# Clearing a scratch tile on GpSimd behind row scatters, and moving a small copy to GpSimd, in a fused FFT filter and mixture-of-experts kernel

## The chip, the cores and the metric

The kernel runs on one core of a Trainium2 chip. The metric is the device time of one execution in microseconds (us). The core has five engines with a program each: TensorE (PE in the profile, its weight loads PEld), VectorE (DVE), ScalarE (ACT), GpSimd (POOL), and SyncE (SP), which here only issues DMA transfers.

## The reference

```python
# x: 8 sequences of 2496 rows of 256; filt: 1249 frequencies of 256
X = np.fft.rfft(x, axis=1)
y = np.fft.irfft(X * (filt_r + 1j * filt_i)[None], n=2496, axis=1)
# 19968 rows go to the one of 8 experts that has the largest logit
logits = y.reshape(19968, 256) @ w_gate
expert_idx = np.argmax(logits, axis=1)
probs = softmax(logits)
for e in range(8):
    mask = expert_idx == e
    h = np.maximum(y[mask] @ w1[e], 0.0)        # 256 -> 1024
    out[mask] = probs[mask, e] * (h @ w2[e])    # 1024 -> 256
```

Everything is float32. Each sequence is filtered along its length, each of its rows is given to one expert, and the expert's two layers are computed on that row alone.

## The kernel before

**The filter.** A sequence of 2496 = 39 x 64 rows is transformed by matrix products, in halves of 128 columns (16 units, two to a sequence). Each unit has five steps t of four small spectra (80 steps in all): transposes on PE (`spec1`, L312), a product by twiddle matrices (`spec2`, L327), the multiplication by the filter on DVE (`filt_`, L346 to L348), the addition of its two parts (`join`, L356, on GpSimd for t < 71, on DVE behind that), and the product back (`spec3`, L367), which ACT copies out (L372). Two scatters of 117 rows each make a pair; a sequence has 11 pairs. For each pair PE transposes (`inv1`, L634, ACT copies to `gh`, L640) and multiplies (`inv2`, L649, ACT copies to `yt`, L651), and `inv3` sends the rows to their expert's place.

**The routing.** `route1` to `route6` work out a sequence's logits, the chosen expert, the gate and the row's place `dest` in a big DRAM array `xs`, sorted by expert. The routing data of each row (`meta`: a tiny constant, the reciprocal of the softmax sum, the row's number) travel with it in four more columns. So a row of `xs` has 260 values of float32. `inv3(b, j, gg)` copies the `meta` of a pair into the last four columns of `yt` (117 x 2 x 4 values, L658, once for a pair) and issues one indirect DMA (L158, `scatter`) for each of its two groups. That makes 22 scatters a sequence, 176 in all. Behind the last sequence eight more scatters (`tail`) fill up each expert's last block with empty rows.

**The experts.** `xs` is worked off in blocks of 128 rows, in three segments: 16 blocks as soon as sequences 0 to 5 lie in `xs` (8 units of two blocks that share an expert's weights), 48 blocks when sequence 7 does (24 units of two), and the rest (up to 99 units of one). A block is loaded (`load`, SP; the first load of a segment waits for all scatters that it needs), scaled (`prep`, DVE, L1048 to L1057), split into two halves of float16 (`split`, ACT L1062 and DVE L1063), transposed by DMA (`turn`, L1070), multiplied by the first layer's weights (`layer1`, 48 matmuls, L1083, with ACT L1089 and L1091 and DVE L1097 in `halves`), by the second's (`layer2`, 24 matmuls, L1109, DVE L1119), scaled by its gate (`out_`, ACT L1125) and scattered to `out` by one more indirect DMA of 128 rows (`send`, also L158). Weights are fetched (`loadw`, L1021, 1 MB each for `wa` and `wb`) when the expert changes. 161 blocks are written out, two stand under a condition and are empty in this run.

**The order.** The order on every engine is set by hand: `at(time, function)` puts each step on a list, which is sorted by its time (in spectral steps t) and issued in this order.

```python
at(t + K["si"] * rho, join, t)
at(t + K["s3"] * rho, spec3, t)
...
z = max(z + 1.2 * c, s0 + c * RT[9] + 0.1 + 0.9 * d * j)
for gg in range(2):
    at(z + 0.45 * d * gg, inv3, b, j, gg)
...
at(nx + 0.95 * dx + 0.5, send, b)
...
for _, f, a in sorted(work, key=lambda w: w[0]):
    f(*a)
```

The first 16 blocks are put among the spectral steps of the last sequences (`PLACE[0]` = 80.9), so that between about 430 and 580 us GpSimd issues scatters of sequences 5 to 7 and of the first blocks' outputs by turns.

Of the kernel before, what the change touches and what calls it, by code (L numbers as in the profile page):

```python
# [9 lines left out]
F32 = mybir.dt.float32  # L10
# [11 lines left out]
S, D, E, F = 2496, 256, 8, 1024  # L22
# [91 lines left out]
def tile_fft_moe(ctx, tc, x, filt_r, filt_i, w_gate, w1, w2, cst, out):  # L114
    nc = tc.nc
    B = x.shape[0]
# [7 lines left out]
    SEG = []  # L124
# [14 lines left out]
    cp = ctx.enter_context(tc.tile_pool(name="cp", bufs=1))  # L139
    ident = cp.tile([128, 128], F32, name="ident")  # L140
    small = cp.tile([128, 64], F32, name="small")
    zrow = cp.tile([128, ROW], F32, name="zrow")
    rbase = cp.tile([128, E], F32, name="rbase0")
    tbs = [cp.tile([128, 4], I32, name=f"tb{i}") for i in range(len(SEG))]
    nblk = cp.tile([128, 1], I32, name="nblk")
# [3 lines left out]
    def free(inst, own, *others):  # L149
        ins = inst.ins  # L150
        for g in (*others, own):
            tc.declare_no_dep(ins, group=g, reason="every row is written once")
        tc.add_to_no_dep_group(own, ins)
        writers.setdefault(own, []).append(ins.name)

    def scatter(dst, idx, src, bound, *groups):
        free(
            nc.gpsimd.indirect_dma_start(  # L158
                out=dst,
                out_offset=bass.IndirectOffsetOnAxis(ap=idx, axis=0),  # L160
                in_=src,
                in_offset=None,
                bounds_check=bound,
                oob_is_err=False,
            ),
            *groups,
        )

    def after(ins, names):
        for name in names:  # L170
            tc.add_manual_dep(
                ins,
                name,
                mybir.DependencyInfo(
                    mybir.DependencyClass.Sync, mybir.DependencyReason.DATA
                ),
                reason="the rows are dispatched",
            )
# [6 lines left out]
    with ExitStack() as fctx:  # L185
# [468 lines left out]
        def inv3(b, j, gg):  # L654
            yt = sti[b, j] if gg == 0 else sti.pop((b, j))
            dest, meta = rst[b]
            if gg == 0:
                nc.vector.tensor_copy(yt[:, :, D:], meta[:, 2 * j : 2 * j + 2])  # L658
            g = 2 * j + gg
            scatter(  # L660
                xs[:, :], dest[:, g : g + 1], yt[:, gg], E * NP - 1,
                f"s{b}", "ld", *(f"s{i}" for i in range(b)),
            )

        def blocks(rb, up, nm):

            t8 = lambda n, dt=F32: rp.tile([128, E], dt, name=nm + n, tag="t" + n)
            ci = t8("ci", I32)
            nb = t8("nb")
            nc.vector.tensor_tensor(nb, rb, small[:, 0:8], op=ALU.subtract)  # L670
            nc.vector.tensor_scalar(ci, nb, up, None, op0=ALU.add)
            nc.vector.tensor_scalar(ci, ci, 7, None, op0=ALU.arith_shift_right)
            nc.vector.tensor_copy(nb, ci)
            return nb
# [168 lines left out]
        def tail(e):  # L843
            scatter(
                xs[:, :], rst["tail"][:, e : e + 1], zrow, E * NP - 1,
                "z", "ld", *(f"s{i}" for i in range(B)),
            )


        K = {"s2": 1.394, "sr": 1.65, "si": 1.85, "s3": 3.6, "f": 0.063, "fd": 0.75, "w": 6.0, "wp": 4.1}  # L850
# [29 lines left out]
        for b in range(B):  # L880
# [26 lines left out]
            for j in range(NPAIR):  # L907
                z = s0 + lead + j * d
                at(z, inv1, b, j)
                at(z + 0.7 * c, inv2, b, j)  # L910
# [3 lines that stand above are left out]
# [9 lines left out]
            if b == B - 1:  # L923
                at(last + 0.1, tails)
                for e in range(E):
                    at(last + 1.2 + e, tail, e)
# [27 lines left out]
        home = []  # L954
# [173 lines left out]
        def send(b):  # L1128
            ot, t = st.pop(b)
            scatter(out[:, :], t, ot, N - 1, "out")  # L1130

# [33 lines left out]
        for b in range(NB):  # L1167
            z, d, s = tau[b]
            y = max(opened(s) + 0.3, z - (1.1 if b else 1.45))
            at(y, prep, b)  # L1170
            at(y + 0.05, split, b)
            at(y + 0.1, turn, b)
            at(z, layer1, b, 0)
            at(z + 0.2 * d, halves, b, 0)
            at(z + 0.25 * d, layer1, b, 1)
            at(z + 0.45 * d, halves, b, 1)
            nx, dx = (tau[b + 1][0], tau[b + 1][1]) if b + 1 < NB else (z + d, d)
            at(nx + 0.5 * dx, layer2, b, 0)
            at(nx + 0.75 * dx, layer2, b, 1)
            at(nx + 0.95 * dx, out_, b)  # L1180
            at(nx + 0.95 * dx + 0.5, send, b)
# [5 lines left out]
        with tc.If(n > NFIN - NREST):  # L1187
            for k in range(nu, len(units)):
                load(k)
                loadw(k, 0)  # L1190
                loadw(k, 1)
            for b in range(NB, NBLK):
                prep(b)
                split(b)
                turn(b)
            for b in range(NB, NBLK):
                for i in range(2):
                    layer1(b, i)
                    halves(b, i)
            for b in range(NB, NBLK):  # L1200
                layer2(b, 0)
                layer2(b, 1)
                out_(b)
                send(b)
# [32 lines left out]
```

## Time and profile before

| | |
|---|---|
| time before, median of 3 runs | 1393.22 us (1393.07 to 1394.41) |
| the profiled execution's own time | 1391.01 us |
| its span, first to last instruction | 1389.2 us |
| mean granted TensorE clock | 0.986 |
| busy: PE / PEld / DVE / ACT / POOL | 1313.8 / 1177.2 / 831.5 / 842.3 / 470.7 us |
| chain that ended last, by line | PE `ph` L1083 24%, PE `po` L1109 24%, DMA `wb` 3%, issue 2% |
| software DMA queue (the scatters) | 19472 packets, 42.51 MB, 12.1% of 16 engines' span |

Busy time is the time in which an engine executes an instruction. The chain is the work that ended last, followed back from the last instruction to what released each step. The granted clock is the share of TensorE's full speed that it was allowed. The 1.8 us between time and span lie ahead of the first and behind the last instruction.

### The profile page before, as it was taken

To read this page: it belongs to the slowest core of one execution; us is meant where nothing else is said; L and a number is where in the kernel's file an instruction comes from. 1 tells how busy PE (TensorE), PEld (TensorE's weight loads), DVE (VectorE), ACT (ScalarE), POOL (GpSimd) and SP (SyncE) were. 2 spreads that over 40 slices of the span, in tenths; PEclk is the share of its full clock that TensorE was granted. 3 is DMA by queue.
4 is the path that set the end of the run, shared out by engine and by line. 5 is a ranking of instruction groups with operands and counts; after the bars stand their busy time and mean duration, and the time that the engine had idled before them with its cause. 6 is when DMAs were issued, how large, how long until landed. Compare 5 with 4: busy or idle time off the path is not lost.

```text
span 1389.2 us, 38966 instructions
## 1 busy us (share of the span) xinstructions
PE 1313.8 (95%) x14855; PEld 1177.2 (85%) x14855; DVE 831.5 (60%) x2400; ACT 842.3 (61%) x1444; POOL 470.7 (34%) x446
## 2 busy tenths in 40 slices
PE   6799999999989899899999999999999999999997
PEld 5778777777877677789999999889999999999997
DVE  1698879888887464255555555555555555555552
ACT  3567667676766555455666665556656565656564
POOL 3638576485664433323111111111111111111111
PEclk9999999999999999999999999999999999999999
DMA  9746565565542722496878878573554546373731
GB/s 173 200 158 206 167 195 178 162 210 171 184 144 81 177 76 79 142 302 172 221 211 212 221 200 248 140 190 73 151 118 106 166 103 167 77 196 73 192 79 43
DMA packets 201438, 220.95 MB, mean 159 GB/s; under 512 B 104359, under 2 KB 177690, under 8 KB 190178
## 3 DMA queue, kind: packets, MB, share of 16 engines
q1 hardware_dynamic: 181310, 175.21, 45.9%
q0 software_dynamic: 19472, 42.51, 12.1%
q8 instruction: 118, 1.93, 0.6%
q10 hardware_dynamic: 468, 0.72, 0.2%
q14 instruction: 70, 0.57, 0.1%
HBM read 335.66 MB, written 61.56 MB: 286 GB/s over the span
## 4 chain that ended last, share of the span: by engine, by line
PE 48%; DMA 5%; issue 2%; DVE 1%; ACT 1%; SPq 1%; POOL 0%; POOLq 0%; ACTq 0%
PE ph L1083 24%; PE po L1109 24%; DMA wb<-wscr 3%; DMA wa<-wscr 1%; DVE bm L1097 1%; DMA T<-xs 0%; POOL out_dram L158 0%; ACT hs L1089 0%; ACT T L1091 0%; DMA xb<-xs 0%; DVE m L1048 0%; ACT xs L1062 0%; SPq L1070 0%; SPq L973 0%; DVE xs L1063 0%
## 5 line engine op out<-in xcount | busy, mean ns | idle before, releaser
L1083 PE MATMUL ph<-T,wa 128*128 128x128 f16 x7728 | 463.8, 220 | 14.1 <-issue 7.4
L1083 PEld LDWEIGHTS <-wa 128*128 128x128 f16 x7728 | 447.5, 98 | 27.2 <-issue 15.6
L1109 PE MATMUL po<-wb,T 128*128 128x256 f16 x2576 | 433.6, 274 | 6.6 <-DMA wb<-wscr 3.6
L1097 DVE TENSOR_TENSOR bm<-hs,T 128x512 f16<-128x512 f32 x322 | 222.7, 692 | 352.8 <-ACT T L1091 308.1
L158 POOL DMA_INDIRECT out_dram<-ot,t x161 | 157.2, 977 | 649.0 <-DVE xs L1063 567.1
L1109 PE MATMUL po<-wb,bm 128*128 128x256 f16 x1288 | 352.2, 273 | 0.0
L1109 PEld LDWEIGHTS <-T 128*128 128x128 f16 x2576 | 246.3, 98 | 38.2 <-issue 7.5
L1089 ACT ACTIVATE hs<-ph 128x512 f32<-128x512 f32 x322 | 191.6, 595 | 104.5 <-PE ph L1083 77.0
L158 POOL DMA_INDIRECT xs<-yt,dest x176 | 186.3, 1059 | 149.8 <-issue 45.7
L1062 ACT ACTIVATE xs<-xb,s 128x256 f16<-128x256 f32 x161 | 81.8, 508 | 226.3 <-DVE s L1052 224.0
L1091 ACT CAST T<-hs 128x512 f16<-128x512 f32 x322 | 199.0, 618 | 10.1
L1109 PEld LDWEIGHTS <-bm 128*128 128x128 f16 x1288 | 126.5, 98 | 15.2
L356 POOL TENSOR_TENSOR p<-tr,ti 128x512 f32<-128x512 f32 x71 | 95.4, 1344 | 85.2 <-DVE ti L348 78.3
L372 ACT COPY U<-pi 128x512 f32<-128x512 f32 (+1 forms) x80 | 87.4, 1093 | 48.9 <-PE pi L367 41.7
L1063 DVE SCALAR_TENSOR_TENSOR xs<-xb,s,xs 128x256 f16<-128x256 f32 x161 | 78.0, 485 | 59.3 <-ACT xs L1062 57.5
L649 PE MATMUL py<-gh,dm 117*117 117x512 f32 x176 | 94.0, 615 | 7.2 <-ACT gh L640 6.8
L367 PE MATMUL pi<-cm,p 128*128 128x128 f32 (+1 forms) x640 | 86.9, 279 | 10.3 <-POOL p L356 7.2
L264 PE MATMUL f<-a,x 117*128 117x117 f32 (+1 forms) x628 | 87.3, 277 | 5.6 <-DVE T L272 2.9
L327 PEld LDWEIGHTS px<-z,bm 128*128 128x128 f32 x640 | 80.0, 193 | 14.2 <-issue 11.5
L367 PEld LDWEIGHTS pi<-cm,p 128*128 128x128 f32 x640 | 79.0, 193 | 12.9 <-POOL p L356 7.9
L272 ACT COPY T<-f 128x468 f32<-128x468 f32 (+1 forms) x80 | 70.7, 884 | 30.5 <-PE f L264 28.8
L327 PE MATMUL px<-z,bm 128*128 128x128 f32 x640 | 87.1, 279 | 0.4 <-ACT U L372 0.4
(180 smaller groups left out, 1326.5 us busy)
## 6 DMA issues: line engine op xcount, KB each, us to landing
wb<-wscr SPq DMA_DIRECT2D x129, 1040.0 KB
wa<-wscr SPq DMA_DIRECT2D x129, 1024.0 KB
xb<-xs SPq DMA_DIRECT2D x161, 130.0 KB
wf<-in_moe_w_dram SPq DMA_DIRECT2D x32, 512.0 KB
x<-in_x_dram SPq DMA_DIRECT2D x210, 78.0 KB
wscr<-wh SPq DMA_DIRECT2D x8, 1040.0 KB
wscr<-wh SPq DMA_DIRECT2D x8, 1024.0 KB
xs<-yt,dest POOLq DMA_INDIRECT x176
```

Source lines behind the costliest of these rows:

```text
L158: nc.gpsimd.indirect_dma_start(out=dst, out_offset=bass.IndirectOffsetOnAxis(ap=idx, axis=0), in_=src, in_offset=None, bounds_check=bound, ...
L264: nc.tensor.matmul(ps[:, n : n + m], lhsT=xt.pop((u, g))[:m], rhs=a1[:m, :m], start=True, stop=True,)
L327: nc.tensor.matmul(ps[:, kk], lhsT=bm[:, 4 * it + kk], rhs=z[:, kk], start=True, stop=True,)
L356: e.tensor_tensor(p, tr, ti, op=ALU.add)
L367: nc.tensor.matmul(ps[:, o : o + n], lhsT=p[:, kk], rhs=cm[:, k, :n], start=True, stop=True)
L372: nc.scalar.copy(U[u % NU].rearrange("p n r -> p r n")[:, r0 : r0 + o // 64, :], ps[:, :o].rearrange("p (r n) -> p r n", n=N2),)
L649: nc.tensor.matmul(ps[:GP], lhsT=dm, rhs=gh[:GP], start=True, stop=True)
L1083: nc.tensor.matmul(ps[:, f], lhsT=w[:, p : p + 128], rhs=xt[:, r, c], start=(n == 0), stop=(n == 5))
L1089: nc.scalar.activation(s, ps, AF.Relu, scale=1.0 / B23)
L1091: nc.scalar.copy(hh, s)
L1097: nc.vector.tensor_tensor(hl, s, hh, op=ALU.subtract)
L1109: nc.tensor.matmul(ps, lhsT=h2[q][:, f % 4], rhs=wv[:, r, f], start=(f == 0 and n == 0), stop=(f == 7 and n == 2),)
```

## The change

A tile `pad` of 128 x 384 float32 is added. `pause()` clears it on GpSimd; nothing reads it. It is issued behind each scatter of sequences 6 and 7 (44), behind each of the eight `tail` scatters, and behind the output scatters of the blocks whose unit is one of the first eight (16 blocks, the first segment). The copy of `meta` into `yt` goes from DVE to GpSimd for all eight sequences (88 copies).

```diff
--- before.py
+++ after.py
@@ -140,6 +140,7 @@
     ident = cp.tile([128, 128], F32, name="ident")
     small = cp.tile([128, 64], F32, name="small")
     zrow = cp.tile([128, ROW], F32, name="zrow")
+    pad = cp.tile([128, 384], F32, name="pad")
     rbase = cp.tile([128, E], F32, name="rbase0")
     tbs = [cp.tile([128, 4], I32, name=f"tb{i}") for i in range(len(SEG))]
     nblk = cp.tile([128, 1], I32, name="nblk")
@@ -165,6 +166,9 @@
             ),
             *groups,
         )
+
+    def pause():
+        nc.gpsimd.memset(pad, 0.0)
 
     def after(ins, names):
         for name in names:
@@ -655,12 +659,14 @@
             yt = sti[b, j] if gg == 0 else sti.pop((b, j))
             dest, meta = rst[b]
             if gg == 0:
-                nc.vector.tensor_copy(yt[:, :, D:], meta[:, 2 * j : 2 * j + 2])
+                nc.gpsimd.tensor_copy(yt[:, :, D:], meta[:, 2 * j : 2 * j + 2])
             g = 2 * j + gg
             scatter(
                 xs[:, :], dest[:, g : g + 1], yt[:, gg], E * NP - 1,
                 f"s{b}", "ld", *(f"s{i}" for i in range(b)),
             )
+            if b >= B - 2:
+                pause()
 
         def blocks(rb, up, nm):
 
@@ -845,6 +851,7 @@
                 xs[:, :], rst["tail"][:, e : e + 1], zrow, E * NP - 1,
                 "z", "ld", *(f"s{i}" for i in range(B)),
             )
+            pause()
 
 
         K = {"s2": 1.394, "sr": 1.65, "si": 1.85, "s3": 3.6, "f": 0.063, "fd": 0.75, "w": 6.0, "wp": 4.1}
@@ -1128,6 +1135,8 @@
         def send(b):
             ot, t = st.pop(b)
             scatter(out[:, :], t, ot, N - 1, "out")
+            if home[b][0] < SEG[0][2]:
+                pause()
```

## Rows read from the trace of the kernel before

**Rows 1.** Part 1 of the page: busy us, share of the span, instructions.

```profile
PE 1313.8 (95%) x14855; PEld 1177.2 (85%) x14855; DVE 831.5 (60%) x2400; ACT 842.3 (61%) x1444; POOL 470.7 (34%) x446
```

**Rows 2.** Waits of PE's weight loads, 430 to 620 us: total us, times, longest.

```profile
PEld L1083 <- issue: 15.6, 28, 1.3
PEld L1109 <- issue: 6.2, 13, 2.2
```

**Rows 3.** The same view, 620 us to the end.

```profile
PEld L1109 <- issue: 1.3, 3, 0.7
```

**Rows 4.** Busy time by stretch: length, PE, PEld, DVE, ACT, POOL, PEclk, DMA, GB/s.

```profile
455.00:468.40 13.40, 8.51 (x42) 5.83 (x41) 7.95 (x23) 5.57 (x9) 6.36 (x7) 0.81 0.57 171
515.70:525.20 9.50, 5.73 (x37) 3.77 (x35) 1.75 (x8) 3.44 (x7) 3.81 (x4) 0.82 0.22 67
556.30:563.30 7.00, 4.55 (x46) 3.85 (x44) 0.78 (x2) 3.03 (x6) 1.97 (x2) 0.76 0.35 97
568.50:576.00 7.50, 4.62 (x31) 3.29 (x29) 1.24 (x3) 2.74 (x5) 2.04 (x3) 0.77 0.54 179
446.50:580.00 133.50, 117.26 (x1182) 95.48 (x1181) 66.31 (x265) 69.95 (x128) 56.92 (x56) 0.94 0.43 111
```

**Rows 5.** Timeline of PE, 514 to 523 us: start, length, instruction, idle before.

```profile
516.68 0.22 PE L1083 MATMUL ph<-T,wa 128*128 128x128 f16 x1 [0.34 <-issue]
...
521.66 0.37 PE L634 MATMUL pg<-ident,U 128*117 128x128 f32 x1 [0.43 <-issue]
```

**Rows 6.** Timeline of GpSimd (POOL), 505 to 524 us.

```profile
511.65 0.99 POOL L158 DMA_INDIRECT xs<-yt,dest  x1 [3.42 <-DMA xs<-yt,dest]
...
519.42 1.00 POOL L158 DMA_INDIRECT xs<-yt,dest  x1 [0.30 <-issue]
```

**Rows 7.** Timeline of GpSimd, 445 to 464 us.

```profile
446.52 0.99 POOL L158 DMA_INDIRECT xs<-yt,dest  x1 [16.32 <-ACT gh L640]
...
462.24 0.99 POOL L158 DMA_INDIRECT xs<-yt,dest  x1 [0.30 <-issue]
```

**Rows 8.** Timeline of GpSimd, 548 to 574 us.

```profile
550.95 0.99 POOL L158 DMA_INDIRECT xs<-yt,dest  x1 [3.59 <-ACT yt L651]
...
557.63 0.99 POOL L158 DMA_INDIRECT out_dram<-ot,t  x1 [0.30 <-issue]
```

**Rows 9.** GpSimd's groups by form: busy us, mean ns, idle before.

```profile
L809 POOL MEMSET go<- 128x176 f32 x1 | 0.2, 236 | 0.0
...
L805 POOL MEMSET wg<- 128x64 f32 x1 | 0.2, 151 | 0.0
```

**Rows 10.** VectorE's (DVE's) groups by form, the copy of line 658.

```profile
L658 DVE COPY yt<-meta 117x8 f32<-117x8 f32 x88 | 28.6, 331 | 0.5
```

**Rows 11.** Timelines of DVE and of GpSimd, 229 to 235 us.

```profile
230.69 1.71 DVE L658 COPY yt<-meta 117x8 f32<-117x8 f32 x1
...
231.06 1.30 POOL L356 TENSOR_TENSOR p<-tr,ti 128x512 f32<-128x512 f32 x1
233.24 1.00 POOL L158 DMA_INDIRECT xs<-yt,dest  x1 [0.88 <-issue]
```

**Rows 12.** Timelines of DVE, GpSimd and PE in sequence 1, 174 to 184 us.

```profile
176.17 0.68 DVE L348 TENSOR_TENSOR ti<-px,ff 64x512 f32<-64x512 f32 x1
...
175.65 1.30 POOL L356 TENSOR_TENSOR p<-tr,ti 128x512 f32<-128x512 f32 x1
177.15 1.00 POOL L158 DMA_INDIRECT xs<-yt,dest  x1 [0.19 <-DVE yt L658]
...
180.75 1.30 POOL L356 TENSOR_TENSOR p<-tr,ti 128x512 f32<-128x512 f32 x1
...
178.84 1.06 PE L367 MATMUL pi<-cm,p 128*128 128x128 f32 x8
```

**Rows 13.** Timeline of GpSimd, and the chain that ended last (start, us), 575 to 590.

```profile
579.22 0.99 POOL L158 DMA_INDIRECT xs<-yt,dest  x1 [0.30 <-issue]
...
586.89 3.66 DMA xb<-xs
```

## The prediction

> **What bounds the kernel now.** I began with the page. PE is busy for 1313.8 of 1389.2 us [rows 1], so an edit on GpSimd (POOL in the profile) can move the end only through time in which PE stands still or runs slowly. The second view is what the weight loads of PE waited for, once between 430 and 620 us, where the last two sequences and the first 16 blocks are interleaved, and once behind that. In the first stretch the layer 1 matmuls (L1083) lose 15.6 us in 28 waits labelled "issue", and those of layer 2 (L1109) another 6.2 us [rows 2]. "Issue" means that the profile shows nothing that PE waited for. In the 769 us behind it, with some 145 blocks of the same matmuls, only 1.3 us of such waits are left [rows 3]. So something belongs to the interleaved stretch alone.
>
> The third view, the timeline of PE, shows the form of such a wait: from 516.68 to 521.66 us single matmuls stand with idle time before each, where the layer's groups otherwise run without a gap [rows 5]. Next I laid GpSimd's timeline beside it. The stall from 515.7 to 521.7 lies inside a run of seven scatters from 511.65 to 519.42, one behind the other, 1.30 us apart (0.99 plus a gap of 0.30) [rows 6]. The other places with such matmuls have a run of scatters too: twelve from 446.52 to 462.24 [rows 7], six from 550.95 to 557.63 with six more close behind [rows 8]. Each stall begins some 4 to 9 us into the run and ends at most about 2 us behind it. Runs of three scatters have none. This is a coincidence in time, four times out of four; the profile names no cause.
>
> What these four places cost is read from one view, busy time by stretch [rows 4]. PE idle: 13.40 - 8.51 = 4.89, 9.50 - 5.73 = 3.77, 7.00 - 4.55 = 2.45, 7.50 - 4.62 = 2.88, together 14.0 us. Behind each idle time the granted clock falls to the lower level for a few us, so the stretches average 0.81, 0.82, 0.76 and 0.77. Length times the missing share is 2.5 + 1.7 + 1.7 + 1.7 = 7.6 us. The four places hold 21.6 us, or 1.6% of the span, and the pauses are put at just these scatters.
>
> **The change part by part.** *The pause.* No memset of 128x384 stands in the trace. Two of the same kind took 236 ns for 176 elements and 151 ns for 64 [rows 9]: 0.76 ns an element, so 236 + 208 x 0.76 = 394 ns. There are 44 behind the scatters of sequences 6 and 7, 8 behind the tails and 16 behind the outputs of the first 16 blocks: 68 x 0.394 = 27 us on GpSimd. A scatter behind a compute instruction started after 0.19 us in place of 0.30 [rows 12], so the distance between two scatters goes from 1.30 to about 0.99 + 0.39 + 0.19 = 1.57 us. The direct cost on the path I set to 0 and bound it so. Between 446.5 and 580 us GpSimd is busy 56.9 of 133.5 us [rows 4]; 55 gaps of 0.30 make it 73 us. The 55 pauses there add 22 us and give back 55 x 0.11 = 6. What waits for the end of these scatters is the first load of the second segment, which is issued at 586.89 us behind the queue's own work [rows 13]; the last scatter of sequence 7 starts at 579.22 and ends 1 us later, so 586.89 - 580.21 = 6.7 us less its landing, which no row gives, are free. Cost of the pauses: 0 to +3 us, taken +1, since the last pair sees one pause between its scatters.
>
> *The gain of the pause.* Bounds: 0, if 1.57 us is still too close, and -21.6 us, if all four stalls go. The nearest rows speak for something between: in sequence 1 three scatters and one addition take 5.1 us, from 175.65 to 180.75 [rows 12], which is 1.7 us a scatter, and PE goes on there with no such stall; at 1.30 us it stalls. 1.57, and more where a copy comes in between, is nearer to 1.7. On the other side GpSimd becomes nearly full where PE gets faster: 73 + 22 - 6 and some 10 us for the copies is 99 us of 133.5 - 21.6 = 112, and a full GpSimd makes long runs again. I take half: -11 us.
>
> *The copy.* 88 copies leave VectorE (DVE): 88 x 331 ns mean = 29 us [rows 10]. The mean holds a few long ones, which run beside GpSimd's work: a copy that began at 230.69 took 1.71 us and ended just behind the addition of GpSimd that had started at 231.06 [rows 11]. DVE doesn't set the end, so I count 0 for it, at most the few us that PE waits for DVE. That DVE and GpSimd shut each other out is what the Trainium skill says (SBUF — State Buffer, "Who interferes with whom"): whichever of a two-port DVE copy and a GpSimd instruction starts first keeps the shared port pair for its whole length. The rows agree, and the same rule speaks against the pauses: each would shut out such a DVE instruction too, which is a rival below.
>
> On GpSimd each copy of 8 elements costs about 0.2 us (the nearest memset is 0.15 to 0.24) and stands ahead of a scatter that must wait for it. How long that wait is, no row shows. Its low bound is the gap of today, 0.19 to 0.30 us [rows 6, 12]; its high bound the 0.84 us between the end of a copy on DVE at 232.40 and its scatter at 233.24 [rows 11]. So a pair costs 0.2 us more at the one and 0.2 + 0.84 - 0.30 = 0.75 at the other. What is queued behind it are the additions (L356), for which PE's matmuls L367 wait. In sequence 1 an addition was ready at 176.85, started at 180.75 and ended at 182.05 [rows 12]; the tightest of the sequence ended at 176.95 and its matmul started at 178.84, so 1.9 us are free there. With 1.4 pairs between two additions (the list sets pairs at most 0.75 of a step apart) and 0.2 us a pair the delay grows by 0.3 us an addition and stays under this for the length of a burst; with 0.75 us it grows by 1.0 and passes it after two to four. I take 0.4 us a pair: nothing on the path, kept up to +6 us (four bursts at 1.5 us) for the range.
>
> *The sum.* The profiled execution took 1391.0 us, its span 1389.2; the median of three is 1393.2, 0.16% above it. 1391.0 - 11 + 1 + 0 = 1381, and 1383 from the median: I say 1382.
>
> **The rivals.** *All of it comes back*: each run is broken up, 1391 - 21.6 = 1369 to 1373. For it: nothing but the four places shows the stall. Against it: GpSimd would stand at nine tenths.
>
> *Nothing comes back*: the stalls are PE's own and only fall beside the runs, or 1.57 us is too close. For it: no row names scatters as the cause, and at 446.52 nine us of scatters went by before PE slowed. The pauses then hide in GpSimd's idle half: 1390 to 1395, no change.
>
> *Slower, by the copy's wait*: the scatter waits on its own engine, at 0.75 us a pair the additions come late in the bursts of sequences 0 to 5, and PE stands in front of L367. Price +6 us, so 1399 if the pause gives nothing; it decides from about 0.6 us a pair. Against it: GpSimd is idle for hundreds of us in all [rows 1], and a burst's delay ends in the next gap; the gain would cover it.
>
> *Slower, by the lock*: each pause holds DVE's small instructions ahead of a transpose. 16 blocks, one pause of 0.39 us each, +6 us, 1399. That is the rule above at its worst; DVE is idle half of that stretch (66.3 of 133.5 busy [rows 4]), which speaks against it.
>
> **How the numbers follow.** A part comes back (1374 to 1389): 0.50. All: 0.13. Nothing: 0.21. Slower by the wait 0.12, by the lock 0.04. What a measurement can tell from no change is about 0.2%, 2.8 us. Faster 0.63, same 0.21, slower 0.16. The range leaves out about a tenth at each end: 1370, most of "all" kept, to 1397, where half of the slower cases lie beyond.
>
> **What would show it.** Right: memsets of about 0.39 us and scatters some 1.57 us apart; the "issue" waits of L1083 between 430 and 620 us well under 15.6 us; fewer short stretches of the lower clock; the first load of the second segment earlier than 586.9. Right on the copy: no L658 on DVE, DVE busy about 29 us less, PE's waits for GpSimd's additions behind 60 us still near 0. Wrong: runs of scatters 1.57 us apart with PE still at one matmul per 0.7 us; waits of L367 for L356 in sequences 0 to 5; or the last scatter of sequence 7 landing behind the queue, so that the segment opens later although PE was faster.

## The result, and the profile after

| | before | after |
|---|---|---|
| median time | 1391.93 us (1389.91 to 1394.41, 6 runs) | 1376.33 us (1370.69 to 1378.48, 6 runs) |
| ratio | | 0.9878, 95% interval 0.9861 to 0.9895 |
| profiled execution: time, span | 1391.01, 1389.2 us | 1377.24, 1375.1 us |

The change saves 15.6 us, 1.2%. The forecast was 1382, range 1370 to 1397.

The first view is again what the weight loads of PE waited for between 430 and 620 us (total us, times, longest). L1090 and L1116 are layer 1 and layer 2 now.

```profile
PEld L1090 <- issue: 8.2, 19, 1.8
PEld L1090 <- DMA T<-xs: 5.9, 2, 4.5
PEld L1116 <- issue: 4.2, 13, 0.6
```

Against [rows 2] the waits for "issue" fell from 15.6 to 8.2 us and from 6.2 to 4.2. A new line stands between them: two waits for the DMA transposes (`T`) of a block. The timeline of PE after the change shows where these are, at the very first matmuls of layer 1:

```profile
467.19 2.84 PE L1090 MATMUL ph<-T,wa 128*128 128x128 f16 x48 [1.58 <-DMA T<-xs]
...
476.62 2.52 PE L1090 MATMUL ph<-T,wa 128*128 128x128 f16 x24 [4.34 <-DMA T<-xs]
```

The third view is GpSimd's timeline, at the place of the second stall:

```profile
517.41 1.02 POOL L159 DMA_INDIRECT xs<-yt,dest  x1 [0.31 <-POOL yt L662]
518.44 0.43 POOL L171 MEMSET pad<- 128x384 f32 x1
519.06 0.99 POOL L159 DMA_INDIRECT xs<-yt,dest  x1 [0.18 <-issue]
...
520.40 0.21 POOL L662 COPY yt<-meta 117x8 f32<-117x8 f32 x1
520.91 1.01 POOL L159 DMA_INDIRECT xs<-yt,dest  x1 [0.30 <-POOL yt L662]
```

Two scatters stand 519.06 - 517.41 = 1.65 us apart, and 520.91 - 519.06 = 1.85 where a copy lies between them. Before it was 1.30 [rows 6]. The stretch as a whole, which answers to the last row of [rows 4] (same columns):

```profile
446.50:580.00 133.50, 125.96 (x1386) 107.31 (x1386) 75.08 (x277) 82.43 (x149) 90.54 (x142) 0.99 0.50 136
```

PE is busy 126.0 in place of 117.3 us of it, at a granted clock of 0.99 in place of 0.94: 8.7 us less idle time, and 133.5 x 0.05 = 6.7 us for the clock. GpSimd is busy 90.5 us in place of 56.9. The sign that had been named for the end of the scatters came too. The first load of the second segment, at 586.89 us before [rows 13], is issued at 572.17 (timeline of SP):

```profile
572.17 0.89 SPq L994 DMA_DIRECT2D xb<-xs  x2
```

To place the gain I read when ACT scales the outputs of a block (L1125, after L1132), since each block has one such instruction. Blocks 4, 5, 8, 10, 11 and 19 before, counted from 0, from the timeline of ACT:

```profile
514.92 0.47 ACT L1125 ACTIVATE ot<-po,g 128x256 f32<-128x256 f32 x1 [2.14 <-issue]
527.24 0.47 ACT L1125 ACTIVATE ot<-po,g 128x256 f32<-128x256 f32 x1 [1.78 <-issue]
...
550.81 0.47 ACT L1125 ACTIVATE ot<-po,g 128x256 f32<-128x256 f32 x1 [0.83 <-DVE g L1119]
...
567.93 0.48 ACT L1125 ACTIVATE ot<-po,g 128x256 f32<-128x256 f32 x1
578.35 0.47 ACT L1125 ACTIVATE ot<-po,g 128x256 f32<-128x256 f32 x1 [0.73 <-DVE t L1057]
...
625.04 0.45 ACT L1125 ACTIVATE ot<-po,g 128x256 f32<-128x256 f32 x1
```

And the same blocks after:

```profile
517.81 0.47 ACT L1132 ACTIVATE ot<-po,g 128x256 f32<-128x256 f32 x1 [2.11 <-issue]
524.65 0.47 ACT L1132 ACTIVATE ot<-po,g 128x256 f32<-128x256 f32 x1 [1.95 <-issue]
...
545.58 0.47 ACT L1132 ACTIVATE ot<-po,g 128x256 f32<-128x256 f32 x1 [0.36 <-issue]
...
558.75 0.48 ACT L1132 ACTIVATE ot<-po,g 128x256 f32<-128x256 f32 x1
564.43 0.47 ACT L1132 ACTIVATE ot<-po,g 128x256 f32<-128x256 f32 x1 [0.68 <-PE po L1116]
...
610.33 0.46 ACT L1132 ACTIVATE ot<-po,g 128x256 f32<-128x256 f32 x1
```

At block 4 the changed kernel is 2.9 us late; at block 5 it is 2.6 early; at block 8, 5.2; at block 10, 9.2; at block 11, 13.9; at block 19, 14.7. From there on the lead stays within 14.0 and 16.2 us. So 17.6 us come back between blocks 4 and 19. At the places of stalls two, three and four it is 5.5 (blocks 4 to 5), 4.0 (8 to 10) and 4.7 us (10 to 11); [rows 4] holds 3.8 + 1.7, 2.5 + 1.7 and 2.9 + 1.7 us for these. The other 3.4 us lie between them and behind the fourth.

The first stall has gone too, but the waits for the first transposes stand in its place. And one thing lies ahead of it: this execution was late already. Shortly before the first stall ACT copies out the one spectral step that is 448 wide and not 512 (L372 before, L376 after):

```profile
450.02 1.00 ACT L372 COPY U<-pi 128x448 f32<-128x448 f32 x1 [0.17 <-PE pi L367]
```

```profile
453.62 1.01 ACT L376 COPY U<-pi 128x448 f32<-128x448 f32 x1 [0.15 <-PE pi L371]
```

That is 3.6 us late, of which 2.9 are left at block 4.

### The profile page after: what moved, and what is told of

It reads as the page before. It is cut to its first block, busy times and chain, and to the rows that moved or that the text cites. A ratio compares the mean times of both kernels' runs of the same rounds, so it can differ in the third digit from the quotient of the medians.

```text
span 1375.1 us, 39054 instructions
## 1 busy us (share of the span) xinstructions
PE 1312.2 (95%) x14855; PEld 1179.1 (86%) x14855; DVE 810.8 (59%) x2312; ACT 846.1 (62%) x1444; POOL 520.5 (38%) x602
## 4 chain that ended last, share of the span: by engine, by line
PE 77%; DMA 9%; DVE 7%; issue 3%; ACT 2%; POOL 1%; SPq 1%; ACTq 0%; POOLq 0%; DVEq 0%
PE ph L1090 27%; PE po L1116 27%; PE py L653 5%; PE f L268 4%; PE px L331 4%; PE pi L371 4%; DMA wb<-wscr 3%; PE pg L638 2%; DMA wa<-wscr 2%; PE pt L316 2%; PE plw L502 2%; DMA U<-in_x_dram 1%; DMA xb<-xs 1%; DVE wm L404 1%; DVE ti L351 1%
## 5 line engine op out<-in xcount | busy, mean ns | idle before, releaser
L1090 PE MATMUL ph<-T,wa 128*128 128x128 f16 x7728 | 460.3, 219 | 14.5 <-DMA T<-xs 7.9
L1090 PEld LDWEIGHTS <-wa 128*128 128x128 f16 x7728 | 445.6, 98 | 26.3 <-DMA wa<-wscr 9.0
L1116 PE MATMUL po<-wb,T 128*128 128x256 f16 x2576 | 431.2, 273 | 4.8 <-DMA wb<-wscr 3.7
L1104 DVE TENSOR_TENSOR bm<-hs,T 128x512 f16<-128x512 f32 x322 | 222.9, 692 | 341.0 <-ACT T L1098 276.8
L1116 PE MATMUL po<-wb,bm 128*128 128x256 f16 x1288 | 351.1, 273 | 0.0
L1116 PEld LDWEIGHTS <-T 128*128 128x128 f16 x2576 | 245.4, 98 | 34.6 <-DMA wb<-wscr 4.7
L159 POOL DMA_INDIRECT xs<-yt,dest x176 | 183.4, 1042 | 77.5 <-issue 28.9
L1116 PEld LDWEIGHTS <-bm 128*128 128x128 f16 x1288 | 126.0, 98 | 15.1 <-issue 0.4
L376 ACT COPY U<-pi 128x512 f32<-128x512 f32 (+1 forms) x80 | 87.4, 1092 | 50.4 <-PE pi L371 39.1
L331 PEld LDWEIGHTS px<-z,bm 128*128 128x128 f32 x640 | 81.1, 195 | 14.2 <-issue 11.3
```

Of the source, the lines that this page charges most:

```text
L159: nc.gpsimd.indirect_dma_start(out=dst, out_offset=bass.IndirectOffsetOnAxis(ap=idx, axis=0), in_=src, in_offset=None, bounds_check=bound, ...
L331: nc.tensor.matmul(ps[:, kk], lhsT=bm[:, 4 * it + kk], rhs=z[:, kk], start=True, stop=True,)
L376: nc.scalar.copy(U[u % NU].rearrange("p n r -> p r n")[:, r0 : r0 + o // 64, :], ps[:, :o].rearrange("p (r n) -> p r n", n=N2),)
L1090: nc.tensor.matmul(ps[:, f], lhsT=w[:, p : p + 128], rhs=xt[:, r, c], start=(n == 0), stop=(n == 5))
L1104: nc.vector.tensor_tensor(hl, s, hh, op=ALU.subtract)
L1116: nc.tensor.matmul(ps, lhsT=h2[q][:, f % 4], rhs=wv[:, r, f], start=(f == 0 and n == 0), stop=(f == 7 and n == 2),)
```

## The experiments

All of them change the new kernel, and each was timed against the kernel before in the same session on the same chip. The time of the same kernel differs between sessions, and this turned out to be the main thing. Each session ran on one chip. Only chip 10 was used twice, and the chip of the result above is not on record, so a chip and a session can't be told apart.

**1. The parts alone.** On chip 10 four kernels ran:

```diff
# e1_pause_only, and the same line in e3, e5, e6, e7, e8, e9
-                nc.gpsimd.tensor_copy(yt[:, :, D:], meta[:, 2 * j : 2 * j + 2])
+                nc.vector.tensor_copy(yt[:, :, D:], meta[:, 2 * j : 2 * j + 2])
# e2_copy_only
-        nc.gpsimd.memset(pad, 0.0)
+        pass
# e3_tiny_pause, e7, e8, e9
-        nc.gpsimd.memset(pad, 0.0)
+        nc.gpsimd.memset(pad[:, :2], 0.0)
# e4_late_copy
-                nc.gpsimd.tensor_copy(yt[:, :, D:], meta[:, 2 * j : 2 * j + 2])
+                (nc.gpsimd if b >= B - 2 else nc.vector).tensor_copy(
+                    yt[:, :, D:], meta[:, 2 * j : 2 * j + 2]
+                )
```

> All pauses stay, the copy goes back to DVE. Theory A (the pauses break up the runs of scatters and so give the gain; the copy on GpSimd costs some us in sequences 0 to 5, where the step at 454 us came 3.7 us later after the change): faster than the full change by 2 to 5 us, so about 1372 against 1392 before, ratio 0.986; scatters 1.60 us apart in every run; the step lateness at 454 us back to within 1 us of before. Rival (the copies between the pairs break the runs up, the pauses do little): 1385 to 1392. Rival (the copy costs nothing, its lateness is scatter between executions): 1376, the same as the full change.

> The copy stays on GpSimd, all pauses are left out. Theory A: the early lateness of some 4 us stays; in the runs of sequences 6 and 7 every second gap holds a copy, so two scatters take 1.30 + 1.80 us, 1.55 us each, which is near to the 1.60 of the pauses for them, while a run of outputs and odd scatters stays at 1.30. If the mean distance decides, a part of the stalls goes: 1384 to 1392. If any GpSimd instruction between two scatters breaks a run, most stalls go: about 1378. If the copies only cost: 1394 to 1397.

> The copy is on DVE, and the pause clears 128x2 elements in place of 128x384, some 0.1 us. Two scatters then stand 0.99 + 0.1 + 0.18 = 1.27 us apart, no more than the 1.30 before. Theory A (the distance in time between scatters decides): the four stalls stay, 1389 to 1393, like before. Rival B (a compute instruction between two scatters is enough, whatever its length): the stalls go as with the long pause, about 1372, like the pauses alone.

> All pauses stay; the copy goes to GpSimd for sequences 6 and 7 alone, and stays on DVE for 0 to 5. Theory A: the early lateness of some 4 us is gone and the late gain stays whole, so about 1372, within 2 us of the pauses alone if the late copies do nothing, 2 to 4 us under them if they help to space the scatters, over them if a fuller GpSimd costs. Rival (the early lateness has another cause): 1376.

| | median us | ratio | 95% |
|---|---|---|---|
| before, chip 10 | 1365.89 (35 runs, 1362.07 to 1372.21) | | |
| e1, pauses alone | 1365.76 | 0.9996 | 0.9979 to 1.0014 |
| e2, copies alone | 1369.69 | 1.0024 | 1.0007 to 1.0041 |
| e3, pause of 128x2 | 1368.95 | 1.0012 | 0.9997 to 1.0027 |
| e4, pauses, copies of sequences 6 and 7 | 1366.11 | 0.9990 | 0.9976 to 1.0005 |

Nothing that had been expected could be read off this, because the kernel before took 1365.9 us here and not 1391.9: what the pauses were to win was not there to be won. Only e2 differs from the kernel before: the copies cost 0.07 to 0.41%. What a copy costs GpSimd is seen in its timeline in e2, in sequence 6:

```profile
450.07 0.99 POOL L159 DMA_INDIRECT xs<-yt,dest  x1 [0.30 <-ACT U L376]
451.06 0.20 POOL L662 COPY yt<-meta 117x8 f32<-117x8 f32 x1
451.56 1.00 POOL L159 DMA_INDIRECT xs<-yt,dest  x1 [0.30 <-POOL yt L662]
452.87 0.98 POOL L159 DMA_INDIRECT xs<-yt,dest  x1 [0.30 <-ACT gh L644]
```

The scatter starts 0.30 us behind its copy, as long as the gap that stands between two scatters anyway. So a pair takes 452.87 - 450.07 = 2.80 us in place of 2.60.

**2. The kernel before and the full change, unchanged, in another session** (chip 5).

> The kernel before, unchanged, with a profile of its own. In the first four experiments the kernel before took 1365.9 us in place of 1391.9, so the runs of scatters alone can't make the stall. Theory D (the stall is a matter of the chip or of what else goes on beside the kernel; a run of scatters only lays it open): where the kernel takes about 1366 us its trace shows the same runs of six to twelve scatters 1.30 us apart, and no place of several single matmuls with idle time before each: PE idle under 3 us in each run where the first trace had 2.5 to 4.9; granted clock at its upper level there; the waits for issue of layer 1 between 430 and 620 us near 8 us in place of 15.6. Where it takes about 1391 us the four stalls are there again. Rival (theory A as it stood, the distance of scatters decides): at 1366 us the runs are already broken up, scatters mostly over 1.5 us apart.

> The full change, unchanged. If the kernel before takes about 1366 us on this chip: theory D and the copy's lateness (copies alone measured 1.0024) give 1369, ratio 1.001 to 1.004, and the gain is gone; if the pauses are worth something by themselves, ratio under 0.999. If the kernel before takes about 1392 us: the ratio 0.988 again.

The kernel before took 1366.28 us (13 runs), the full change 1365.78, ratio 1.0003 (0.9981 to 1.0024), just under the 1.001 to 1.004 that had been expected. The profiled execution of the kernel before took 1372.32 us. Its GpSimd timeline at the second place, the busy time there and the waits of PE's weight loads between 430 and 620 us:

```profile
508.20 0.99 POOL L158 DMA_INDIRECT xs<-yt,dest  x1 [3.24 <-DMA xs<-yt,dest]
...
515.99 1.00 POOL L158 DMA_INDIRECT xs<-yt,dest  x1 [0.30 <-issue]
```

```profile
507.50:517.00 9.50, 9.50 (x112) 8.43 (x110) 5.64 (x29) 6.43 (x13) 6.97 (x7) 1.00 0.33 94
```

```profile
PEld L1083 <- issue: 7.1, 18, 1.3
...
PEld L1083 <- DMA T<-xs: 4.2, 1, 4.2
```

The run of seven scatters is there, 1.30 us apart within a hundredth, as in [rows 6]. But PE is busy for 9.50 of 9.50 us at the full clock, where it was 5.73 of 9.50 at 0.82 [rows 4]. Of the waits for "issue" 7.1 us are left, which is what the interleaved stretch has of them without a stall. And the wait for the first transposes (4.2 us) stands here in the kernel before too. It is no cost of the change: it is what comes next when the first stall is away. So a run of scatters doesn't make the stall by itself. Something that differs between sessions or chips has to be added.

**3. The price of pauses**, on chip 10 again (kernel before 1368.06 us), with a second look at the short pause:

```diff
# e5_triple_pause
         nc.gpsimd.memset(pad, 0.0)
+        nc.gpsimd.memset(pad, 0.0)
+        nc.gpsimd.memset(pad, 0.0)
# e6_pause_all
-            if b >= B - 2:
-                pause()
+            pause()
```

> Copy on DVE, each of the 68 pauses clears the tile three times, so some 1.2 us in place of 0.43; two scatters stand 0.99 + 1.2 + 0.18 = 2.4 us apart. It measures the price of a pause. Between 445 and 570 us 55 scatters and outputs would take 55 x 2.4 = 130 us in place of 125, so GpSimd has no idle time left there and the last scatter of sequence 7 comes some 10 us late; the first load of the second segment waits for it. Theory (a pause is free as long as GpSimd keeps idle time, and costs as soon as it is full): slower by 5 to 15 us than the kernel before where that takes 1366, ratio 1.004 to 1.011. Rival (the pauses cost nothing at any length, the wait has more slack than that): ratio 1.000. Where the kernel before takes 1391 us on this chip, the stalls go and the price is taken off the gain: 0.987 to 0.995.

> Copy on DVE, one pause behind each scatter of all eight sequences (176) and of the tails and first outputs. GpSimd gets 132 more pauses of 0.43 us in 90 to 430 us, where it was busy 220 of 340 us and PE waits for its additions. By the price of the copies (about 0.5 us a pair on GpSimd, 3 to 4 us on the path in all) a pair costs 2 x (0.43 - 0.12) = 0.6 us more here: slower than the kernel before by 3 to 8 us, ratio 1.002 to 1.006 where that takes 1366. Rival (what makes the copies cost is the scatter's wait for the copy, not time on GpSimd): ratio 1.000.

> The pause of 128x2 elements again (copy on DVE), for the case that the kernel before takes some 1391 us on this chip: then theory A (distance) leaves the stalls, 1389 to 1393, and rival B (any compute instruction between) takes them away, about 1370. Where the kernel before takes about 1366, this run can't tell the two apart and gives 1365 to 1372.

e5 took 1404.52 us, ratio 1.0256 (1.0213 to 1.0299): 36 us slower, where 5 to 15 were expected. The scatters stand 2.8 to 2.9 us apart and not 2.4. Timeline of GpSimd, memsets left out:

```profile
568.64 1.00 POOL L159 DMA_INDIRECT xs<-yt,dest  x1 [0.40 <-issue]
...
571.51 0.99 POOL L159 DMA_INDIRECT xs<-yt,dest  x1 [0.48 <-issue]
```

The chain that ended last goes through the last scatter of sequence 7 and the first load of the second segment, which had been named as what would be late next:

```profile
599.75 2.71 DMA xs<-yt,dest
...
602.80 2.17 DMA xb<-xs
```

No trace of the kernel before was taken beside e5. In its trace from chip 5, which has no stall either, that scatter starts at 560.40 and the load is issued at 567.59 (timeline of SP):

```profile
567.59 0.34 SPq L987 DMA_DIRECT2D xb<-xs  x1
```

So the load comes 602.80 - 567.59 = 35.2 us late, about the whole of the 36 us. PE stands for most of the difference in one piece. The profile names ACT's output instruction, for the split of the segment's first block stands ahead of that on ACT. Timeline of PE:

```profile
608.13 0.58 PE L1118 MATMUL po<-wb,T 128*128 128x256 f16 x2 [21.82 <-ACT ot L1134]
```

The chain has one number more that the prediction lacked: the scatter's landing takes 2.71 us from its start. By it, 586.89 - 579.22 - 2.71 = 5.0 us were free in [rows 13].

e6 took 1379.63 us, ratio 1.0086 (1.0060 to 1.0111): 11.6 us slower, where 3 to 8 were expected. PE did not stand where I had looked for it, in front of L367, but in the routing. Waits of PE between 90 and 455 us in e6, and below them the same line in e1:

```profile
PE pp L579 <- DVE oh L570: 8.0, 5, 2.1
```

```profile
PE pp L579 <- DVE oh L570: 0.2, 1, 0.2
```

The timelines of DVE and GpSimd in e6 at one of the five places:

```profile
206.35 2.93 DVE L569 TENSOR_TENSOR oh<-eq,rmx 117x176 bf16<-117x176 f32 x1
...
206.46 1.29 POOL L360 TENSOR_TENSOR p<-tr,ti 128x512 f32<-128x512 f32 x1
...
207.79 1.28 POOL L360 TENSOR_TENSOR p<-tr,ti 128x512 f32<-128x512 f32 x1
```

In e1 the same instruction took 0.93 us beside one addition, and 0.34 where none runs beside it (434.01). Timeline of DVE in e1:

```profile
203.63 0.93 DVE L569 TENSOR_TENSOR oh<-eq,rmx 117x176 bf16<-117x176 f32 x1
```

In e6 the pauses have made GpSimd late, two of its additions come one behind the other just when DVE works out `oh`, and DVE is held until both are done (207.79 + 1.28 = 209.07; 206.35 + 2.93 = 209.28). At a second of the five places `oh` takes 2.97 us. At the other three it takes 0.34 and is only late, since the two additions meet an instruction ahead of it: `eq` (L565; 3.03 and 3.22 us, in e1's timeline 0.34) twice, and L475 (4.26 us, 1.28 at 152.24) once:

```profile
265.07 3.03 DVE L565 SCALAR_TENSOR_TENSOR eq<-lg,small 117x176 f32<-117x176 f32 x1
```

The Trainium skill says it so (SBUF — State Buffer, "Who interferes with whom"): a DVE instruction with two inputs in SBUF contends with a GpSimd instruction that reads SBUF, not with one that only writes it. The trace agrees with both halves. The addition reads, and holds DVE. A pause only writes, and of the 322 instructions of DVE's largest group with two inputs (`bm`, L1104 after) 24 run beside a pause; none of the 322 takes over 725 ns, and the mean of 692 ns is that of before.

e7 took 1371.03 us once beside 1368.06, as expected for a session without the stall.

**4. In search of the stall.** Two more sessions, on chip 0 and on chip 13.

> The pause of 128x2 elements (copy on DVE) in another session, to meet the stall again. Two sessions of the kernel before gave 1390 to 1394 us, three gave 1362 to 1374. If the kernel before takes some 1391 us here: theory A (the distance in time decides) 1389 to 1393 with the four stalls in the trace, rival B (any compute instruction between two scatters) about 1370 without them. If it takes about 1366: the stall doesn't show and this run gives 1365 to 1372 too, which only adds to the count of sessions without it.

> The pause of 128x2 elements in one more session (so far: chips 10, 5, 10 and 0 without the stall). If the kernel before takes some 1391 us here: theory A (distance in time) 1389 to 1393, rival B (any compute instruction between two scatters) about 1370. If it takes about 1366: ratio 0.998 to 1.002.

> The full change in the same session. If the kernel before takes some 1391 us here: ratio 0.988 as in the result. If it takes about 1366: 0.998 to 1.003, pauses free and copies worth 0 to 4 us, as in the session on chip 5 (1.0003).

| | chip | before us | this us | ratio | 95% |
|---|---|---|---|---|---|
| e8, pause of 128x2 | 0 | 1365.98 | 1365.91 | 1.0001 | 0.9982 to 1.0020 |
| e9, pause of 128x2 | 13 | 1389.65 (11 runs) | 1391.37 | 1.0012 | 0.9993 to 1.0031 |
| e10, the full change | 13 | 1389.65 | 1373.33 | 0.9879 | 0.9843 to 0.9915 |

The session on chip 13 has the stall, and there the two theories come apart. GpSimd in e9 at the second place, and PE beside it:

```profile
515.77 1.00 POOL L159 DMA_INDIRECT xs<-yt,dest  x1 [0.19 <-issue]
516.78 0.11 POOL L171 MEMSET pad<- 128x2 f32 x1
517.08 0.99 POOL L159 DMA_INDIRECT xs<-yt,dest  x1 [0.18 <-issue]
```

```profile
518.84 0.22 PE L1090 MATMUL ph<-T,wa 128*128 128x128 f16 x1 [1.02 <-issue]
...
520.27 0.27 PE L638 MATMUL pg<-ident,U 128*117 128x128 f32 x1 [1.04 <-issue]
520.99 0.27 PE L638 MATMUL pg<-ident,U 128*117 128x128 f32 x1 [0.45 <-issue]
```

There is a memset between every two scatters, and still they stand 1.31 us apart, since the shorter gap (0.19 for 0.30) pays for the memset. PE stalls at the same work and in the same form as in [rows 5]. With the full change on the same chip the waits for "issue" of layer 1 fall from 13.0 to 8.4 us (weight loads, 430 to 620 us, e9 and then e10):

```profile
PEld L1090 <- issue: 13.0, 27, 1.5
```

```profile
PEld L1090 <- issue: 8.4, 20, 1.7
```

So a compute instruction between two scatters is not enough. With 1.31 us between the starts the stall stays, and so it does in the first place of the kernel before, where the twelve scatters [rows 7] stand 15.72 / 11 = 1.43 us apart in the mean; with the full change (1.65 and 1.85 us) it goes. That the spacing does it is the nearest reading, but it is not shown: e10 differs from e9 by the length of the pause and by the place of the copies, which takes them off DVE too. Neither was changed alone in a session with the stall.

## Why the prediction was right, point by point

**What bounds the kernel.** The four places were rightly read as one thing, tied to runs of scatters and worth about 21.6 us, though 1.9 of the first one's 4.9 us of idle time are a wait for ACT's `gh`. Stalls two to four gave back what [rows 4] holds for them, within 0.2 us each. The kernel before on chip 5, where the runs are there and the stalls are not, has a span 18.7 us shorter than that of [rows 1] (1389.2 - 1370.5). What one trace could not show is that the stall belongs to some sessions. That the forecast was put to the test in one of these was luck: on chip 5 the ratio was 1.0003.

**The pause.** Its length was put at 394 ns and is 438 ns in the mean (29.8 us for 68); the distance was put at 1.57 us and is 1.65. Its price of +1 us was near enough: e1 shows none, -0.21 to +0.14%. That the price is hidden by GpSimd's idle time is shown by e5, which used this up and paid 36 us at the very load that had been named.

**The gain** is the term that was mis-sized: -11 us forecast, -17.6 us measured between blocks 4 and 19. Less the 2.9 us that block 4 was late, 14.7 us of it were left, and 1391.0 - 1377.2 = 13.8 us between the profiled executions (15.6 between the medians). I took half of 21.6 because a GpSimd that is nearly full makes long runs again. It did: after the change GpSimd is busy 90.5 of 133.5 us, and its longest run has 25 scatters (513.73 to 555.12 us). But that run, at 1.65 us and more between most starts, has no stall in it, so the reason for the half was wrong. What took something off the full 21.6 us lay elsewhere. The first stall's 7.4 us (4.9 idle and 2.5 of clock) were mostly replaced by 5.9 us of waiting for the first transposes, and 0.7 came back. And 3.6 us were lost ahead of it. These need not belong to the change: the same step stands at 448.06 and 448.02 us in the two kernels on chip 5, and at 451.14 (e9) and 450.82 (e10) on chip 13. So 14.2 + 3.4 + 0.7 us came back, and 3.6 ahead of the stalls and 0.9 behind block 19 were lost, which leaves 13.8. That the total came near the forecast owes something to these two losses, which the prediction had not named.

**The copy.** I took 0.4 us a pair between bounds of 0.2 and 0.75. It is near the low bound: 0.2 us in e2's timeline, 0.30 in the mean of the 88 after the change (26.3 us), and the scatter's wait for its own engine costs nothing over the gap of before. DVE is busy 831.5 - 810.8 = 20.7 us less, where 29 were named. The effect on the time lies between none (after_again, 1.0003) and 0.07 to 0.41% (e2). Whether the copy costs anything at all stays open; 0 was a fair term.

**The rivals.** *All of it comes back* (1369 to 1373) was nearer than it had been given credit for: 15.6 us came back in the result and 1389.65 - 1373.33 = 16.3 on chip 13, of 21.6. *Nothing comes back* is what chip 5 shows for the full change (1.0003) and chip 10 for the pauses alone (0.9996), but for another reason than the rival's: there the stalls don't exist, so nothing was lost that could come back. With the short pause, where scatters stand 1.3 us apart, layer 1 has 7.0 us of "issue" waits on chip 10 (e3) and 7.1 on chip 0 (e8), as in the kernel before on chip 5. The full pause never ran on chip 0. *Slower by the copy's wait* was to decide from about 0.6 us a pair at +6 us. e6 put 2 x (1.61 - 1.30) = 0.6 us on each pair and cost 11.6 us, so the threshold stood about right and the price was too low by half, for it was paid at another place (the routing's `oh`). *Slower by the lock* of the pauses didn't come, but not because pauses hold nothing on DVE. A copy of `meta` that runs beside nothing takes 0.16 to 0.17 us there; in e1 one took 0.45 us, from 454.44 to 454.89, beside a pause from 454.41 to 454.85 (timeline of DVE):

```profile
454.44 0.45 DVE L662 COPY yt<-meta 117x8 f32<-117x8 f32 x1
```

At 0.3 us a case this is small, e1 was no slower than the kernel before, and the full change takes these copies off DVE. The prediction's row for the lock [rows 11] agrees only in part with the rule beside it: the copy began at 230.69, ahead of the addition at 231.06, and yet it was the copy that waited.

**Still open.** Why some sessions have the stall: the traces show the same runs of scatters, the same instructions and nothing that PE waited for. What exactly is late in it was not found. Among the DMA queues the profile lists two of the kind `instruction`, which would be a suspect. But from 568.50 to 576.00 us, the stretch of the fourth stall, they move nothing; these are all the queues that do (the DMA view of the kernel before):

```profile
q1 hardware_dynamic: 144, 1.05, 43.6%
q0 software_dynamic: 176, 0.29, 10.3%
```

Also the shares of pause and copy in spacing the scatters were never taken apart in a session with the stall; e1 and e2 ran where there was none. And the four stalls are not the whole difference between sessions. The kernel before took 1391.9 and 1366.3 us, 25.6 apart; the full change still took 1376.3 and 1373.3 where there are stalls, and 1365.8 on chip 5. These 7.5 to 10.5 us were not looked into.

## What to carry to other kernels

When an engine stalls without a releaser, lay the other engines' timelines beside it, and look for what goes on there at the same time; then test the coincidence by changing its spacing and not only its presence. Take the kernel before along in every session: the full change gained 1.2% in two sessions and nothing in a third, and only the time of the kernel before told which case it was. Padding an engine is free only while it has idle time up to the load that waits for it, so work out how much that is before choosing the length.

## What the runs showed of the hardware

The same program took 1390 to 1394 us in two sessions and 1385 to 1394 us on chip 13, but 1362 to 1374 us on chips 10, 5 and 0, with the same 1.30 us between scatters in both traces of the kernel before. The stalls on PE have a step of their own: in e9 single matmuls come 0.72 us apart (520.27, 520.99), and in the timeline of [rows 5] those from 516.68 to 521.66 us stand one step of 0.71 us apart or two (the starts between are 518.11, 518.82, 519.54, 520.25 and 520.96), while the scatters beside them come 1.30 us apart. And a DVE instruction of 0.34 us took 0.93 us beside one addition of GpSimd, and 2.93 beside two.
